# A new order of the work words in a Mamba-2 scan followed by a low-rank mixer

## The chip, the cores and the metric

The kernel runs on one core of one Trainium2 chip. Its time is the device time of one execution in microseconds; for the kernel before, three runs gave 214.86 (median), 214.03 and 215.4. The profile comes from one further execution on the chip, taken by the hardware profiler, so its span is not one of these three times.

## The reference, cut to what matters

```python
# attention: batch 4, heads 8, sequence 768, head_dim 32, state 16, chunks of 32
for c in range(nc):
    la  = log_a[:, :, sl];  cum = np.cumsum(la, axis=-1)
    L   = np.exp(cum[..., :, None] - cum[..., None, :]) * causal
    M   = einsum('bhin,bhjn->bhij', Cc, Bc) * L
    y[:, :, sl] = einsum('bhij,bhjd->bhid', M, xc) \
                + einsum('bhin,bhnd->bhid', Cc, state) * exp(cum)
    state = exp(sum(la)) * state + sum_j(Bc * xc * exp(cum[-1] - cum))
# bridge: (batch, heads, seq, head_dim) -> x of (batch, 768, 256)
# mixer: U 768x32, V 32x768, w_ch1 256x1024, w_ch2 1024x256
h  = x.T @ U @ V
u  = x + h.T
return u + relu(u @ w_ch1) @ w_ch2
```

U, V and both w arrive as float64; everything else is float32.

## The kernel before

**How the work is cut.** A batch's 768 tokens are three pairs of 128-token blocks, so there are 12 pairs over the four batches. The scan goes pair by pair; the mixer goes batch by batch, and within a batch in three blocks of 256 tokens.

**What sets the order.** The kernel is one long list of words. `PLANS[1]`, a string of 547 words (lines 40 to 72), is read by `follow` (lines 1063 to 1082) from left to right, and each word issues the instructions of one step on whatever engines the step uses. The program is under manual scheduling, so each engine runs its instructions in the order in which the words stand; waits between engines come from the data. Moving a word therefore moves its instructions in the queues of TensorE, VectorE, ScalarE, GpSimd and SyncE at once. `PLANS[0]` holds the loads that are issued first: B, C and x of the pairs 0 to 2.

**How to read a word.** In the words of the scan, the first number is an offset: -3, -2, -1 are the pairs 0 to 2 (batch 0), 0 to 2 the pairs 3 to 5, 3 to 5 the pairs 6 to 8, 6 to 8 the pairs 9 to 11. In the words of the mixer the first number is a lag: 1 is batch 0, then 0, -1 and -2 are the batches 1 to 3.

- Loads, all on SyncE's queue: `B` (B and C of a pair), `X` (x of a pair), `L` (both), `Z0` and `Z1` (U and V), `w0` and `w1` (the halves of w1's first quarter), `w2` to `w4` (its other quarters), `w5` to `w8` (the four pieces of w2). A load by `B`, `X`, `w` or `L` is held until the last VectorE instruction ahead of its word is done: `follow` sets `until[:] = [vector.last]`, and `begin` (line 195) hangs the first DMA on it. `Z` is not held.
- `c`, the conversion of float64 words to float32 (`to_fp32`, lines 402 to 436), in three passes, one for each time the word stands: two VectorE operations and one ScalarE copy; one ScalarE operation; three VectorE operations. `c0` is U and V, `c1` and `c2` are the halves of w1's first quarter, `c3` to `c5` its other quarters, `c6` to `c9` the pieces of w2. `R` refines a converted piece into three parts for products in a faster format.
- The scan: `A`, `K` (decays), `P`, `Q` (B and C scaled, into `BC`; `Q` is one block), `D`, `E` (B decayed, into `bd`), `V`, `T` (transposes of `BC` into `T` and `Cm`; from pair 6 on by VectorE's own transposes, a trip through DRAM, `squares`, and back), `g` (the products of C and B), `m`, `M` (the causal mask on them, one half each), `s` (the pair's state sums), `u` (the running state `S`), `n` (products within a chunk), `i`, `j` (products with the state), `y` (copies of the result into `yT`), `t`, `O` (the result with tokens on partitions, `ytok`; late pairs by the same kind of trip).
- The mixer: `v` spreads U and V, `p` is x.T U (line 803, copied to `pT` on line 808), `x` the product with V (line 815), `a` adds it to `yT`, `S` splits a block of u into three parts, `U` is a plain float32 product of a block with one quarter of w1 (for the first two blocks of batch 0), `f`, `e`, `h` are the first, second and third step of the same product in three parts, `d` is one piece of the product with w2, with the last sum and the store in its last pieces.
- `F` is a run of idle matmuls.

All VectorE operations go through one recording helper, so they all show as line 170. In `inter` (the words `i` and `j`), a tiny VectorE copy, `settled`, is put in ahead of the products where no earlier instruction is at hand to order them after others (`apart`).

**Where the change acts.** The words of the start run up to the first product with w1, those of the second stage until two blocks have met all of w1, then come dense products of the batches 0 and 1 with the scan of later pairs between them, then the last pairs' scan and the mixing of batch 2 (`p-1`, `x-1`, `a-1`, `S-1`), then the products of the last two batches.

Of the kernel before, what the change touches and what calls it, by code (L numbers as in the profile page):

```python
# [71 lines left out]
}


# [1041 lines left out]
```

## The time and the profile before

| | |
|---|---|
| median of three runs | 214.86 us (214.03 to 215.4) |
| span of the profiled execution | 212.4 us |
| instructions | 7511 |
| TensorE matmul | 202.9 us busy (96%) |
| TensorE weight load | 180.9 us (85%) |
| VectorE | 173.2 us (82%) |
| ScalarE | 121.0 us (57%) |
| GpSimd | 6.3 us (3%) |
| DMA | 21.43 MB, 101 GB/s on average |
| chain that ended last | TensorE 75%, VectorE 8%, issue 4%, DMA 4% of the span |

The profiled execution's own time is its span, 212.4 us; the timed runs are 2.46 us above it by their median, and contain whatever lies around the span. A busy share is a mean over stages with different limits, so the table says that TensorE is nearly always occupied, and not what each stage waits for. In the views, PE is a matmul, PEld a weight load, DVE VectorE, ACT ScalarE and SPq a transfer issued by SyncE; a row of a timeline begins with the start and the duration in microseconds, and ends with the idle time before it and what released it, where there was some.

### The profile page before, as it was taken

Reading aid. Unit: us, or ns where it says so; the run is one execution under the profiler, and the core shown is the slowest. Engines: PE = TensorE matmul, PEld = TensorE weight load, DVE = VectorE, ACT = ScalarE, POOL = GpSimd, SP = SyncE. Lnnn points to the kernel's source line nnn. Section 1 sums busy time; section 2 is a strip of 40 time slices with the busy share of each in tenths; the row PEclk is TensorE's granted clock in tenths of the full one; section 3 lists DMA queues with packets and bytes.
Section 4 is the critical chain, followed back from the end, with each engine's and each line's share of the span. In section 5 each row is a group of like instructions: output and inputs, shape, how many; then the busy total and the mean of one; then the engine's idle time right before and its main releaser. Section 6 shows DMA issues by size and latency. Waiting matters only on the chain.

```text
span 212.4 us, 7511 instructions
## 1 busy us (share of the span) xinstructions
PE 202.9 (96%) x3190; PEld 180.9 (85%) x3190; DVE 173.2 (82%) x363; ACT 121.0 (57%) x279; POOL 6.3 (3%) x22
## 2 busy tenths in 40 slices
PE   7988889999999999999999999899999999999994
PEld 5765666878979997988999999589998999999993
DVE  4299979999899999999799995777986299859941
ACT  3354668489969746285588361669713565554310
POOL 4022000000000000000000000000000000000000
PEclk9999999999999999999999999999999999999999
DMA  5997799994751488356755766626510000324354
GB/s 82 138 150 160 89 246 181 190 241 121 102 71 31 79 207 130 88 83 83 108 89 94 149 143 132 112 38 122 117 52 0 0 5 0 49 32 71 49 102 99
DMA packets 120177, 21.43 MB, mean 101 GB/s; under 512 B 110096, under 2 KB 118352, under 8 KB 120144
## 3 DMA queue, kind: packets, MB, share of 16 engines
q1 hardware_dynamic: 120144, 20.95, 53.9%
q8 instruction: 25, 0.41, 0.9%
q14 instruction: 8, 0.07, 0.2%
HBM read 14.39 MB, written 6.55 MB: 99 GB/s over the span
## 4 chain that ended last, share of the span: by engine, by line
PE 75%; DVE 8%; issue 4%; DMA 4%; ACT 3%; SPq 3%; POOL 0%; POOLq 0%; DVEq 0%; ACTq 0%
PE x L846 35%; PE z L846 28%; DMA bc<-in_B_dram 4%; SPq L196 3%; DVE words L170 2%; PE x L584 2%; PE z L739 1%; PE w L803 1%; PE x L714 1%; PE x L739 1%; DVE S L170 1%; ACT yT L759 1%; PE x L815 1%; DVE o L170 1%; DVE BC L170 1%
## 5 line engine op out<-in xcount | busy, mean ns | idle before, releaser
L170 DVE SCALAR_TENSOR_TENSOR words<-words 128x512 fp32r<-128x512 f32 (+6 forms) x60 | 39.4, 669 | 2.4 <-ACT words L420 0.8
L846 PE MATMUL x<-words,w 128*128 128x256 f32 x288 | 38.1, 280 | 0.0
L846 PEld LDWEIGHTS x<-words,w 128*128 128x128 f32 x288 | 34.9, 188 | 1.6 <-issue 1.2
L846 PE MATMUL x<-u,w 128*128 128x256 f32 x240 | 34.3, 282 | 0.0
L846 PE MATMUL z<-u,w 128*128 128x256 f32 x240 | 32.7, 278 | 0.0
L851 ACT ACTIVATE x<-x 128x512 f32<-128x512 f32 (+1 forms) x27 | 15.5, 577 | 28.2 <-PE x L846 26.4
L846 PEld LDWEIGHTS x<-u,w 128*128 128x128 f32 x240 | 30.3, 188 | 0.6 <-ACT yT L759 0.2
L846 PEld LDWEIGHTS z<-u,w 128*128 128x128 f32 x240 | 29.7, 188 | 0.1
L851 ACT ACTIVATE z<-z 128x512 f32<-128x512 f32 (+1 forms) x24 | 13.7, 574 | 12.3 <-PE z L846 10.2
L846 PE MATMUL z<-words,w 128*128 128x256 f32 x144 | 19.6, 280 | 0.0
L846 PEld LDWEIGHTS z<-words,w 128*128 128x128 f32 x144 | 17.7, 188 | 0.9 <-issue 0.9
L170 DVE SCALAR_TENSOR_TENSOR words<-x,words 128x512 fp32r<-128x512 f32 x20 | 13.6, 682 | 4.5 <-ACT words L886 4.4
L170 DVE SCALAR_TENSOR_TENSOR words<-z,words 128x512 fp32r<-128x512 f32 x20 | 13.6, 682 | 2.2 <-ACT words L886 2.2
L886 ACT ACTIVATE words<-x 128x512 fp32r<-128x512 f32 x20 | 12.0, 598 | 3.3 <-PE x L846 3.2
L170 DVE TENSOR_TENSOR yT<-x,yT 128x384 f32<-128x384 f32 (+1 forms) x15 | 9.2, 613 | 5.1 <-PE x L846 2.7
L170 DVE TENSOR_TENSOR BC<-bc,F 128x512 f32<-128x512 f32 (+2 forms) x18 | 8.7, 508 | 5.4 <-DMA bc<-in_B_dram 3.0
L886 ACT ACTIVATE words<-z 128x512 fp32r<-128x512 f32 x20 | 11.8, 597 | 1.7 <-PE x L846 1.2
L170 DVE SCALAR_TENSOR_TENSOR S<-S,kept,w 128x64 f32<-128x64 f32 x40 | 11.2, 279 | 1.7
L584 PE MATMUL x<-Cm,T 32*64 32x128 f32 x192 | 11.6, 307 | 0.6 <-DVE Cm L170 0.4
L651 ACT ACTIVATE Sm<-S,slot 128x128 f32<-128x128 f32 (+1 forms) x18 | 6.0, 385 | 9.9 <-DVE S L170 9.9
L584 PE MATMUL z<-Cm,T 32*64 32x128 f32 x192 | 10.5, 307 | 0.0
L170 DVE TENSOR_TENSOR M<-x,causal 128x256 int32<-128x256 int32 x24 | 9.1, 421 | 1.6 <-PE z L584 1.6
(152 smaller groups left out, 363.5 us busy)
## 6 DMA issues: line engine op xcount, KB each, us to landing
words<-in_moe_w_ch_dram SPq DMA_DIRECT2D x7, 512.0 KB, 5.5
squares<-w1f SPq DMA_DIRECT2D x52, 64.0 KB, 1.9
x<-in_x_dram SPq DMA_DIRECT2D x24, 128.0 KB, 4.1
out_dram<-o SPq DMA_DIRECT2D x32, 64.0 KB, 2.3
bc<-in_B_dram SPq DMA_DIRECT2D x24, 64.0 KB, 3.5
bc<-in_C_dram SPq DMA_DIRECT2D x12, 128.0 KB, 3.9
T<-squares SPq DMA_DIRECT2D x6, 256.0 KB, 4.3
ytok<-squares SPq DMA_DIRECT2D x6, 256.0 KB, 3.6
```

The source lines that it names most:

```text
L170: self.last = call(*args, **kwargs)
L196: op = nc.sync.dma_start(**kwargs)
L584: nc.tensor.matmul(out=g[r][cols, c], lhsT=s["T"][rows, 0, c, cols], rhs=s["Cm"][rows, :, :, ts(2 * c + p, Q)].rearrange("r v t i -> r v i ...
L651: nc.scalar.activation(s["Sm"][:, sl, v], s["S"][:, sl, ts(v, D)], AF.Copy, scale=slot[:, v, None])
L714: product = nc.tensor.matmul(out=y[r // 2][p][ts(v, H), c], lhsT=own[ts(r, Q)], rhs=s["T"][ts(r, Q), 1, :, ts(2 * c + p, Q)].rearrange("r ...
L739: product = nc.tensor.matmul(out=y[n][p][ts(v, Q), c], lhsT=x_sb[k][half, c, h], rhs=s["M"][half, h // 2, c, h % 2], start=fresh(k, n, p, ...
L759: nc.scalar.copy(out=yp[ts(1 - v, H), n, :, p], in_=y[n][p][ts(v, H)])
L803: nc.tensor.matmul(out=p[ts(n, H)], lhsT=UU[:, c].rearrange("p t r -> p (t r)"), rhs=ytok[b][:, c, ts(n, P)], start=(c == 0), stop=(c == N ...
L815: nc.tensor.matmul(out=h[q][:, :VS], lhsT=pT[rows], rhs=V4[rows], start=True, stop=True, skip_group_check=True)
L846: nc.tensor.matmul(out=t, lhsT=lhsT, rhs=rhs, start=start, stop=True, skip_group_check=True)
L851: nc.scalar.activation(t, t, AF.Copy, scale=1.0 + EPS)
L886: nc.scalar.activation(gs[j, i][0], t, AF.Relu, scale=NEAR)
```

## The change

The 547 words are the same, in a new order; no function is touched. U and V (`Z0`, `Z1`) are loaded later, behind the second pair's state words, and w1's first half quarter (`w0`) earlier; w1's third quarter (`w3`, `c4`) is loaded and converted ahead of its second and fourth, and `U1.0.2`, the product with it, is the first product with w1. Between the dense pieces `d0.1` and `d0.2` of batch 1 stand more words of the last pairs, and the words `p-1` and `x-1` come closer to the last of them. The pieces of the last two batches are interleaved in another way. As `i` and `j` lie differently, one more `settled` copy is issued (three, from two); otherwise every kind of instruction occurs as often as before.

The loads and conversions of the start, and the words around them (the rest of the string down to `d1.0` cut):

```diff
-        'Z1 F5 A0 Q-3.0 Q-3.1 A1 Q-3.2 F4 V-3.0.0 Q-2.1 V-3.1.5 K2 D-3 g-3 Q-2.2 Q-2.0 V-2.0.2 '
-        'Z0 m-3 M-3 F2 V-2.1.2 Q-1.2 E-1.0 s-3 Q-1.0 D-2 n-3 w0 Q-1.1 V-1.0.2 u-3 F1 V-1.1.3 s-2 '
-        'w1 i-3 g-2 u-2 j-3 y-3 F2 g-1 i-2 B3 B4 B5 w2 w3 X3 w4 X4 m-2 M-2 w5 c0 c0 m-1 B6 O-3.0 '
-        'c0 M-1 w6 E-1.1 n-2 s-1 u-1 c2 v0 w7 c1 c2 j-2 i-1 y-2 j-1 n-1 c1 y-1 P0 D0 c1 T0 c2 '
-        't-2 O-1.3 P2 X5 T0 X6 w8 P1 D2 p1.0.4 p1.4.6 c3 c3 x1 a1.0 a1.1 T1 T2 T2 T1 g0 U1.0.0 '
-        'c3 c4 c4 U1.0.1 g1 m0 M0 c5 c4 m1 M1 c5 D1 s0 u0 U1.1.0 U1.1.1 U1.1.2 i0 n0 y0 c6 c6 s1 '
-        'c5 g2 c7 u1 R2 m2 c7 U1.1.3 M2 c8 c8 c7 U1.0.2 L4 U1.0.3 i1 n1 y1 c6 R1 R0 c8 R5 c9 s2 '
-        'c9 c9 n2 d1.0 L5 R6 u2 R0 d1.1 P3 S1.2 d1.0 R7 d1.0 i2 y2 R3 t1 R1 t0 R2 R5 d1.1 R4 P4 '
...
+        'F5 A0 Q-3.0 Q-3.1 A1 Q-3.2 F4 V-3.0.0 V-3.1.5 Q-2.1 w0 Q-2.2 K2 g-3 D-3 s-3 Q-2.0 D-2 '
+        'V-2.0.2 F2 V-2.1.2 Z0 g-2 E-1.0 m-3 M-3 s-2 u-3 Q-1.2 w1 Q-1.0 V-1.0.2 Q-1.1 E-1.1 m-2 n-3 '
+        'i-3 u-2 Z1 c1 w3 B3 c1 B4 B5 M-2 i-2 n-2 c1 j-3 c2 c0 c0 X3 y-3 F1 V-1.1.3 s-1 j-2 F2 g-1 '
+        'c0 y-2 v0 t-2 u-1 O-3.0 m-1 M-1 c4 c4 c2 i-1 j-1 P0 n-1 D0 p1.0.4 y-1 c4 O-1.3 w2 p1.4.6 P1 '
+        'T0 c2 T0 w4 x1 w5 T1 a1.0 T1 a1.1 g0 U1.0.2 m0 M0 P2 X4 w6 D1 c3 s0 c3 U1.0.0 u0 g1 T2 X5 '
+        'w7 c3 w8 R0 L5 m1 D2 M1 T2 c5 c6 U1.1.0 c5 U1.0.1 s1 i0 n0 y0 c6 c5 R2 u1 U1.1.1 B6 c7 '
+        'U1.0.3 s2 c6 u2 R1 g2 R3 c7 c8 c8 U1.1.2 m2 M2 c7 R5 c8 U1.1.3 c9 n2 i2 S1.2 y2 d1.0 d1.1 '
+        'c9 i1 R4 n1 c9 L4 P3 D3 R0 T3 d1.0 d1.0 R2 y1 R3 X6 d1.0 t0 f1.2.2 P4 f1.2.0 R1 f1.2.3 '
...
```

The place of `n3` to `n5`, where a wait for a mask can arise:

```diff
-        'f0.0.1 e0.0.0 T5 f0.0.2 f0.0.3 d1.2 D4 s4 e0.0.1 u3 e0.0.2 e0.0.3 L7 L8 D5 s5 h0.0.0 i3 '
-        'n3 y3 d0.0 d0.0 u4 h0.0.1 g5 h0.0.2 u5 d0.0 d0.0 d0.0 h0.0.3 d0.0 m5 M5 d0.0 P6 d0.0 T6 '
-        'n4 S0.1 i4 y4 d0.0 D6 d0.0 d0.0 d0.0 D8 f0.1.2 P7 T7 S0.2 f0.1.3 s6 n5 i5 y5 e0.1.2 '
...
+        'f0.0.0 M4 f0.0.1 e0.0.3 d1.2 e0.0.0 e0.0.1 u5 d1.1 i3 n3 n4 i4 d0.0 y3 L8 h0.0.2 h0.0.3 '
+        'h0.0.0 y4 h0.0.1 d0.0 d0.0 d0.0 P6 S0.1 d0.0 g5 m5 d0.0 M5 f0.1.1 T6 n5 S0.2 i5 P7 y5 d0.0 '
```

The last pairs and the mixing of batch 2:

```diff
-        'd0.1 d0.2 h0.2.2 d0.1 d0.1 d0.1 d0.2 d0.2 d0.2 h0.1.1 d0.1 t4 T7 d0.0 P8 T8 s7 u7 g6 m6 '
-        'd0.1 M6 t5 d0.1 d0.2 d0.1 d0.2 d0.2 d0.2 d0.1 d0.1 d0.1 d0.1 s8 u8 n6 i6 y6 p-1 g7 T8 '
-        'd0.2 x-1 d0.1 m7 M7 n7 a-1.0 a-1.1 S-1.0 i7 y7 g8 f-1.0.2 f-1.0.3 m8 M8 n8 i8 y8 t6 t7 '
-        'S-1.1 e-1.0.2 h-1.0.2 t6 e-1.0.3 f-1.0.0 f-1.0.1 h-1.0.3 t8 f-1.1.3 e-1.0.0 e-1.0.1 '
...
+        'd0.2 d0.1 d0.2 d0.2 d0.2 T8 u6 g7 s7 d0.1 d0.0 m7 D8 M7 d0.2 d0.1 u7 d0.1 d0.1 d0.2 g6 s8 '
+        'm6 T8 M6 d0.1 d0.2 d0.2 n6 u8 d0.2 p-1 i6 x-1 n7 d0.2 i7 y6 a-1.0 a-1.1 S-1.0 y7 t6 g8 m8 '
+        'f-1.0.0 f-1.0.1 M8 e-1.0.0 n8 i8 y8 t7 S-1.1 e-1.0.1 f-1.0.2 f-1.0.3 t8 f-1.1.2 f-1.1.1 '
...
```

The order of the first loads behind the first three pairs was V, U, w0, w1, B3, B4, B5, w2, w3, X3, w4, X4, w5, B6, w6, w7, X5, X6, w8, and is w0, U, w1, V, w3, B3, B4, B5, X3, w2, w4, w5, X4, w6, X5, w7, w8, the load of pair 8, B6. The plain products with w1 stood as U1.0.0, U1.0.1, U1.1.0, U1.1.1, U1.1.2, U1.1.3, U1.0.2, U1.0.3, and stand as U1.0.2, U1.0.0, U1.1.0, U1.0.1, U1.1.1, U1.0.3, U1.1.2, U1.1.3.

35 rows, old and new, of the table PLANS are left out of this document.

## The prediction

> **What bounds the kernel now.** I read the page first (engine shares, queues), then a table of busy time by stage, then the timelines of VectorE, ScalarE and SyncE where a stage showed slack.
>
> ```profile
> span 212.4 us, 7511 instructions
> PE 202.9 (96%) x3190; PEld 180.9 (85%) x3190; DVE 173.2 (82%) x363; ACT 121.0 (57%) x279; POOL 6.3 (3%) x22
> ...
> q8 instruction: 25, 0.41, 0.9%
> ```
>
> TensorE's bar fills 96% of the span, but a bar also covers waiting of small matmuls, so the share says little before the stages are taken apart. The stages below are mine: up to the first product with w1, up to the state where all of w1 has been multiplied for two blocks, the dense middle, the hole at 130, the dense end, the tail.
>
> ```profile
> core 0: us, PE busy (x) PEld busy (x) DVE busy (x) ACT busy (x) POOL busy (x), PEclk, DMA share, GB/s
> 0.00:33.80 33.80, 29.02 (x626) 21.47 (x626) 24.72 (x78) 17.96 (x48) 6.27 (x22) 1.00 0.86 147
> 33.80:62.30 28.50, 27.87 (x502) 22.54 (x497) 26.80 (x62) 21.38 (x49) 0.00 (x0) 1.00 0.74 150
> 62.30:130.10 67.80, 67.58 (x1061) 62.42 (x1060) 62.64 (x123) 42.25 (x99) 0.00 (x0) 1.00 0.60 107
> 130.10:139.10 9.00, 8.29 (x305) 5.88 (x304) 7.19 (x16) 5.04 (x17) 0.00 (x0) 1.00 0.65 126
> 139.10:209.30 70.20, 70.14 (x709) 68.55 (x704) 51.41 (x87) 34.39 (x69) 0.00 (x0) 1.00 0.26 49
> 209.30:212.40 3.10, 0.00 (x0) 0.00 (x0) 0.40 (x1) 0.00 (x0) 0.00 (x0) 0.94 0.41 109
> ```
>
> Weight loads (second number) show density better than matmuls: 62.42 of 67.80 in the middle (92%) and 68.55 of 70.20 at the end, but 5.88 of 9.00 in the hole and 21.47 of 33.80 at the start. A new order of the same instructions can win only where TensorE is not dense: the start (bound by VectorE and the transfers, DMA share 0.86), the second stage (VectorE 26.80 of 28.50, TensorE 27.87: both near full) and the hole. The clock is 1.00 until TensorE's work ends (0.94 in the tail), so no term comes from it. The last 3.10 us belong to the last sum and store, which the new order leaves last.
>
> **The change part by part.** The 547 words are the same ones; nothing is added but one tiny copy (`settled`), as the pairs j and i lie differently. So every term is a wait or a place in a queue.
>
> *Start, on VectorE's queue.* The chain that ends at a1.0 (the first sum into the mixer's input) passes through VectorE:
>
> ```profile
> 9.95 0.29 DVE L170 TENSOR_TENSOR BC<-bc,F 128x128 f32<-128x128 f32 x1 [1.59 <-DMA bc<-in_B_dram]
> 10.16 0.60 DVE L170 TENSOR_SCALAR Cm<-w,slot 128x128 f32<-128x128 f32 x2
> ...
> 16.18 1.30 DVE L170 SCALAR_TENSOR_TENSOR S<-S,kept,w 128x64 f32<-128x64 f32 x4
> 17.40 0.14 DVE L170 COPY settled<-slot 128x1 f32<-128x1 f32 x1
> ...
> 24.86 0.69 DVE L170 TENSOR_TENSOR BC<-bc,F 128x512 f32<-128x512 f32 x1
> ...
> 29.84 1.29 DVE L170 TENSOR_TENSOR BC<-bc,F 128x512 f32<-128x512 f32 x2 [1.36 <-DMA bc<-in_B_dram]
> 31.05 0.42 DVE L170 TENSOR_TENSOR bd<-bc,FD 128x256 f32<-128x256 f32 x1
> 31.39 0.76 DVE L170 TENSOR_SCALAR words<-words 128x512 int32<-128x512 int32 x2
> 32.06 0.55 DVE L170 TENSOR_TENSOR yT<-x,yT 128x384 f32<-128x384 f32 x1
> ...
> 33.92 1.29 DVE L170 SCALAR_TENSOR_TENSOR words<-words 128x512 f32<-128x512 f32 x2
> 35.24 0.69 DVE L170 SCALAR_TENSOR_TENSOR w1f<-words 128x512 f32<-128x512 f32 x1
> ```
>
> Out of the queue ahead of a1.0 go: the 0.60 of V-3.1.5's copies, which now stand before Q-2.1 and run inside its wait of 1.59; P2 and with it the wait of 1.36 for B5 (P2 takes half of the 1.29, 0.65); D2, 0.42; c3's first pass, 0.76. Together 3.79. Into it come: c4 whole, by c3's rows 0.76 + 1.29 + 0.69 = 2.74; the `settled` copy, 0.14; and a new wait, c1's first pass for w0. Its price follows from SyncE's queue:
>
> ```profile
> 13.05 0.58 SPq L196 DMA_DIRECT2D words<-in_moe_V_dram  x1
> ...
> 17.57 0.37 SPq L196 DMA_DIRECT2D bc<-in_B_dram  x1
> ```
> ```profile
> words<-in_moe_w_ch_dram SPq DMA_DIRECT2D x7, 512.0 KB, 5.5
> ...
> words<-in_moe_w_ch_dram SPq DMA_DIRECT2D x2, 256.0 KB, 4.6
> ```
>
> w0 takes V's place at 13.05 and lands 4.6 later, at 17.65. VectorE is there after u-2, which ended at 17.40 and now ends some 0.5 sooner (the 0.60, less a little overlap), so it stands still for about 0.7, and M-2, the rest of c1, j-3, c2 and c0 queue behind it. Bounds: 0 if w0 lands before 16.9, 1.5 if it needs the 5.5 us of the larger pieces. I take 0.7, because the row is that of the same transfer. In: 3.58; out: 3.79; a1.0 starts at 31.9 instead of 32.06, and VectorE has 2.74 - 1.83 = 0.9 more of its work behind it there. U, V sooner or later costs nothing by itself: c0's last pass feeds v0, and V4 is first read by x1, some 6 us after.
>
> *Second stage.* U1.0.2 can start right behind a1.1, where U1.0.0 did (33.8), as c4 is done; U1.0.0 and U1.1.0 need c1, c2, which are done too, so c3 and c5 get their time behind dense work. VectorE's lead is then 0.9, and one more wait in front of c9 may go:
>
> ```profile
> 57.42 1.30 DVE L170 SCALAR_TENSOR_TENSOR words<-words 128x512 f32<-128x512 f32 x2 [0.80 <-ACT words L420]
> ```
>
> In the new order S-1.2 stands before c9's last pass and covers ScalarE's part of c9. But TensorE itself has only 28.50 - 27.87 = 0.63 to give here. The gain lies between 0 and 0.63; I take 0.5, as the first half of VectorE's lead is enough for it.
>
> *Middle.* 67.58 of 67.80: TensorE is full, another order gains nothing by this row. The pairs n-3, n-4 now stand back to back, and n-5 behind f0.1.1 must wait for M5, which has S0.1 before it: a wait of some 0.7 by VectorE's queue, against small waits now. I take 0, and -1 to +1 as bounds.
>
> *The hole at 130.* Here the old order has used up its dense products before the last pairs' attention and the next batch's mixing, which are chains:
>
> ```profile
> 130.13 0.43 PE L619 MATMUL w<-x,bd 64*32 64x64 f32 x24
> ...
> 131.19 0.28 PE L714 MATMUL x<-T,Sm 32*64 32x64 f32 x2
> ...
> 131.62 1.59 PE L803 MATMUL w<-ytok,UU 128*64 128x128 f32 x24
> ...
> 135.00 0.59 PE L815 MATMUL x<-V,pT 32*128 32x384 f32 x2 [0.61 <-ACT pT L808]
> ```
> ```profile
> 133.13 0.27 ACT L761 COPY yT<-x 128x128 f32<-128x128 f32 x1 [0.63 <-DVE o L170]
> ...
> 134.68 0.27 ACT L808 COPY pT<-w 128x128 f32<-128x128 f32 x1
> 135.31 0.91 ACT L551 ACTIVATE Cm<-T,slot 128x256 f32<-128x256 f32 x2 [0.36 <-DMA T<-squares]
> ```
> ```profile
> 124.20 0.71 DVE L170 STREAM_TRANSPOSE w1f<-BC 128x512 f32<-128x512 f32 x1
> ...
> 131.74 1.30 DVE L170 STREAM_TRANSPOSE o<-yT 128x512 f32<-128x512 f32 x2
> ...
> 135.95 0.56 DVE L170 TENSOR_TENSOR yT<-x,yT 128x384 f32<-128x384 f32 x1
> ...
> 137.81 0.68 DVE L170 TENSOR_TENSOR u<-yT,u 128x512 fp32r<-128x512 f32 x1
> ```
>
> At the density of the middle the 5.88 us of loads would need 5.88 / 0.92 = 6.4; the hole costs 9.0 - 6.4 = 2.6. One piece is plain: pT is ready to be copied at 133.2, but ScalarE does y6's six copies first, and these wait for VectorE's output transposes (131.74). In the new order pT's copy stands before y6; g7, s7, g6, s8 and n6 have d0.1 and d0.2 pieces between and behind them. What is left bare behind the last d0.2 is p-1, i6, x-1, n7, i7, g8: the 6.4 less s8 and n6 (131.19 - 130.13 = 1.06) and g7 (0.8, an estimate: half of p-1's 1.59, as its rows were not separated), so 4.5. The chain beside it: p-1 1.59, pT 0.27, x-1 to the first sum 0.95 (135.00 to 135.95), the four sums 1.86 (135.95 to 137.81), the far half of the split 0.68: 5.35 until f-1.0.0 can run through. Slack 0.85 instead of 2.6: a gain of 1.75. Bounds: 0 if T8's round trip is late (below), 2.6 if nothing waits.
>
> *Instruction blocks.* The order is said to follow their arrival. q8's 25 packets and 0.41 MB are blocks of 16 KB, and TensorE's loads do wait where nothing else ends the wait:
>
> ```profile
> PEld x L714 <- issue: 1.5, 5, 0.3
> ...
> PEld x L846 <- issue: 1.4, 5, 0.5
> PEld x L739 <- issue: 1.3, 3, 0.6
> ```
>
> These are 4.2 us at most over the span, mostly in waits of 0.3. I put no term on them: they lie in the start, where VectorE's chain ends last anyway, and inside stages already counted. [...]
>
> *Sum.* Start -0.2, of which nothing counts twice as U1.0.2 is tied to a1.1; second stage -0.5; middle 0; hole -1.75; end 0 (68.55 of 70.20 is dense). Together -2.4: the span goes from 212.4 to 210.0. This execution is profiled; the median of the three timed runs is 214.86, 2.46 above its span, so the forecast is 212.5.
>
> **The rivals.**
> - *The stream of transfers slips* (slower). w3 is put ahead of B3, and waits until c1's first pass is done (18.2: w0's 17.65 and some 0.6, an estimate from c3's 0.76 on twice the columns), where B3 went out at 17.57; 512 KB at 147 GB/s are 3.6 us before it. B3 leaves 1.2 later and lands 3.5 to 4.8 later, P0 (24.86) then waits to 28 or more, and D0, c4's last pass, the ytok copy, P1 and a1 stand behind it on VectorE; w2, w4 and w5 wait for these in turn, so c3 and c5 are late as well. It decides when P0 waits over 1.5. Price: 3 to 4 at U1.0.1, partly made up: +3.0, and if the hole's gain halves, 214.9 + 3.0 - 0.9 = 217. For it: DMA share 0.86. Against: VectorE now has the whole of c4's first pass and M-1 before P0, so 1 us of lateness is free.
> - *The hole stays.* T8 now takes 135.31 + 0.91 - 124.20 = 12.0 from its transposes to its Cm; in the new order about 10.5 us of TensorE's words lie between T8 and g8. If the trip takes 12.0 again, g8 and what follows it waits 1.5, and the gain falls to 0.25: 214.0. For it: T8's stores share SyncE with the outputs of d0.0, which come right behind. Against: in the old order those outputs stood before T8's stores.
> - *Blocks count.* If the 4.2 of issue waits are real and half go, 212.5 - 2.1 = 210.4. Against: the dense middle shows few of them.
>
> **How the numbers follow.** Forecast 0.37 (211.3 to 213.5), hole stays 0.30, slip 0.21, blocks 0.12. A difference under 1%, 2.1 us, is about what a measurement here cannot tell from none. Faster by over 1% (below 212.7): 0.22 of the forecast's own range and tails, the blocks' 0.12, and 0.06 from better cases of the hole: 0.42 with rounding. Slower (above 217.0): 0.18. Within: 0.40. The range takes the blocks' case at its low end less a little and the slip's at its high: 209.6 to 217.2.
>
> **What would show it.** Right: a1.0 near 31.9 with no long wait before P0; U1.0.2 near 33.8; no wait for c9; from the last d0.2 to f-1.0.0 about 5.4 us, with pT's copy ahead of y6's. Wrong: an idle VectorE before BC at 25 to 28 (slip); g8 waiting for Cm behind a landing of T (hole); a stage from 62 to 130 that lasts over 1 us longer than 67.8, which I have put at 0.

## The result, and the profile after

The new order is slower: 218.25 us against 215.13 us (medians of four executions each), a ratio of 1.015 with a 95% interval of 1.010 to 1.020. The forecast was 212.5 us, its range 209.6 to 217.2. A second comparison (a0_new, below) gave 1.019 (1.011 to 1.027). Ratios, and medians of spans further down, leave out executions more than 1.5% above the fastest of the same kernel beside them. The profiled execution's span is 216.1 us against 212.4, so 3.7 us have to be found. Both spans lie at the low end of what was timed: wherever a run lists the time and the span of one execution, they are 1.66 to 1.98 us apart. So 212.4 belongs to a time of some 214.1 us (of the 2.46 that the prediction put between span and median, some 0.7 was only this), and 216.1 to the fastest of the new order's four, 217.82.

The page of the new order, its first lines and TensorE's clock over 40 slices, in tenths of full speed:

```profile
span 216.1 us, 7539 instructions
PE 205.5 (95%) x3190; PEld 181.3 (84%) x3190; DVE 174.0 (81%) x364; ACT 121.7 (56%) x279; POOL 6.5 (3%) x22
...
PEclk9988589999999999999999999999999999999999
...
q8 instruction: 25, 0.41, 0.9%
```

One row is new: the granted clock. In the old order it was 1.00 up to the tail; here it falls in two places, from 15.0 to 18.3 us and from 21.8 to 28.6. The bars of the matmuls are 2.6 us longer (205.5 against 202.9) at the same 3190 instructions, while VectorE and ScalarE have nearly the same (174.0 against 173.2, 121.7 against 121.0). The view of busy time by stretch, of the new order and then of the old one, with the same columns as in the prediction:

```profile
10.00:15.00 5.00, 2.46 (x86) 1.60 (x77) 4.69 (x14) 1.95 (x7) 1.23 (x3) 0.99 0.99 105
15.00:18.40 3.40, 3.40 (x138) 2.39 (x122) 3.23 (x11) 1.33 (x5) 1.30 (x3) 0.51 1.03 253
18.40:21.80 3.40, 2.31 (x100) 1.84 (x92) 3.34 (x11) 1.66 (x4) 0.35 (x1) 0.99 0.59 182
21.80:28.30 6.50, 6.32 (x97) 3.91 (x96) 5.00 (x15) 2.96 (x9) 0.51 (x1) 0.50 0.88 110
28.30:33.80 5.50, 4.98 (x132) 3.81 (x131) 4.21 (x9) 3.88 (x9) 0.00 (x0) 0.97 0.71 85
```
```profile
10.00:15.00 5.00, 3.92 (x141) 2.92 (x140) 4.79 (x17) 2.16 (x8) 1.67 (x3) 1.00 1.05 130
...
18.40:21.80 3.40, 2.77 (x102) 1.95 (x108) 3.35 (x10) 2.40 (x6) 0.13 (x1) 1.00 0.61 91
21.80:28.30 6.50, 5.86 (x209) 4.56 (x191) 6.32 (x20) 4.17 (x14) 0.51 (x1) 1.00 0.81 100
```

From 21.8 to 28.3 us TensorE runs at 0.50 of its clock. Its bar is nearly full there (6.32 of 6.50) with 97 matmuls instead of 209, and it is now VectorE that waits (5.00 busy instead of 6.32). Who waits for whom is in VectorE's and ScalarE's timelines:

```profile
22.71 0.14 DVE L169 COPY settled<-slot 128x1 f32<-128x1 f32 x1
...
25.91 0.76 DVE L169 TENSOR_TENSOR M<-x,causal 128x256 int32<-128x256 int32 x2 [0.70 <-PE z L583]
...
29.47 0.15 DVE L169 COPY settled<-slot 128x1 f32<-128x1 f32 x1 [1.48 <-PE z L713]
29.58 0.69 DVE L169 TENSOR_TENSOR BC<-bc,F 128x512 f32<-128x512 f32 x1
...
35.00 0.56 DVE L169 TENSOR_TENSOR yT<-x,yT 128x384 f32<-128x384 f32 x1 [0.23 <-PE z L814]
```
```profile
27.40 0.32 ACT L1015 COPY V<-x 128x192 f32<-128x192 f32 x1 [2.47 <-PE z L1011]
```

P0 (`BC`) starts at 29.58, and not because B3 is late: ahead of it the copy `settled` waits 1.48 us for TensorE. The first sum of a1.0 starts at 35.00 instead of the old order's 32.06, and the first product with w1 follows. The rows that date the rest, from TensorE's timelines of the new and of the old order (the first product with w1, the first piece of d1.0, i7, the first product behind g8, and the last products):

```profile
36.79 0.70 PE L845 MATMUL x<-yT,w1f 128*128 128x256 f32 x2
...
57.05 1.99 PE L845 MATMUL x<-words,o 128*128 128x256 f32 x8
...
140.26 0.28 PE L713 MATMUL x<-T,Sm 32*64 32x64 f32 x2
...
141.99 1.18 PE L845 MATMUL x<-u,w 128*128 128x256 f32 x8
...
211.65 1.10 PE L845 MATMUL z<-w,words 128*128 128x256 f32 x8
```
```profile
33.84 1.99 PE L846 MATMUL x<-yT,w1f 128*128 128x256 f32 x8
...
54.76 1.99 PE L846 MATMUL x<-words,o 128*128 128x256 f32 x8
...
137.38 0.28 PE L714 MATMUL x<-T,Sm 32*64 32x64 f32 x2
...
139.11 1.06 PE L846 MATMUL x<-u,w 128*128 128x256 f32 x7
...
208.17 1.07 PE L846 MATMUL z<-w,words 128*128 128x256 f32 x8
```

The old order's first product stood at 33.84 (in the experiment b1_pt, whose start is the old one, at 33.83). Against it the new order is 2.95 us late at the first product, 2.29 at the first d1.0 (57.05 - 54.76), 2.53 at i3 (97.48 - 94.95), 2.88 at i7 and at the first product behind g8, 3.51 at the end of the last product (212.75 - 209.24), and 3.7 at the end of the span. At i3, at i7 and at the end TensorE has the same words behind it in both orders. At the first d1.0 it has not: the old order has done n1 by then, and the new one does it later (from 61.16 to 61.97), so 2.29 flatters the new order by some 0.8.

### The profile page after: what moved, and what is told of

Read it like the earlier page. It is cut to its first block, busy times and chain, and to the rows that moved or that the text cites. A ratio compares the mean times of both kernels' runs of the same rounds, so it can differ in the third digit from the quotient of the medians.

```text
span 216.1 us, 7539 instructions
## 1 busy us (share of the span) xinstructions
PE 205.5 (95%) x3190; PEld 181.3 (84%) x3190; DVE 174.0 (81%) x364; ACT 121.7 (56%) x279; POOL 6.5 (3%) x22
## 4 chain that ended last, share of the span: by engine, by line
PE 83%; DVE 6%; ACT 3%; DMA 3%; SPq 2%; issue 1%; DVEq 0%
PE x L845 36%; PE z L845 28%; PE x L583 3%; SPq L195 2%; DMA bc<-in_B_dram 2%; PE w L618 2%; PE z L738 2%; PE x L814 2%; DMA T<-squares 1%; PE x L713 1%; PE w L802 1%; PE x L738 1%; DVE BC L169 1%; DVE M L169 1%; PE w L768 1%; PE z L713 1%
## 5 line engine op out<-in xcount | busy, mean ns | idle before, releaser
L845 PE MATMUL x<-words,w 128*128 128x256 f32 x288 | 40.0, 280 | 0.0
L845 PEld LDWEIGHTS x<-words,w 128*128 128x128 f32 x288 | 35.7, 188 | 1.5 <-issue 1.2
L845 PE MATMUL z<-u,w 128*128 128x256 f32 x240 | 34.2, 280 | 0.0
L845 PEld LDWEIGHTS z<-u,w 128*128 128x128 f32 x240 | 30.4, 188 | 0.2
L845 PE MATMUL z<-words,w 128*128 128x256 f32 x144 | 21.2, 281 | 0.0
L845 PEld LDWEIGHTS z<-words,w 128*128 128x128 f32 x144 | 18.4, 188 | 0.9 <-issue 0.7
L169 DVE TENSOR_TENSOR u<-yT,u 128x512 fp32r<-128x512 f32 x10 | 6.9, 686 | 7.8 <-ACT u L839 7.6
L583 PE MATMUL x<-Cm,T 32*64 32x128 f32 x192 | 11.0, 322 | 1.4 <-ACT Cm L507 1.0
L169 DVE TENSOR_TENSOR BC<-bc,F 128x512 f32<-128x512 f32 (+2 forms) x18 | 9.9, 566 | 2.0 <-ACT F L371 1.3
L550 ACT ACTIVATE Cm<-T,slot 128x256 f32<-128x256 f32 x12 | 5.4, 500 | 9.8 <-DMA T<-squares 9.8
```

The costliest lines, as they stand in the source:

```text
L169: self.last = call(*args, **kwargs)
L550: nc.scalar.activation(s["Cm"][:, i], s["T"][:, 1], AF.Copy, scale=slot[:, i, None])
L583: nc.tensor.matmul(out=g[r][cols, c], lhsT=s["T"][rows, 0, c, cols], rhs=s["Cm"][rows, :, :, ts(2 * c + p, Q)].rearrange("r v t i -> r v i ...
L845: nc.tensor.matmul(out=t, lhsT=lhsT, rhs=rhs, start=start, stop=True, skip_group_check=True)
```

## The experiments

Each kernel was timed in turn with the old order on the same chip; ratios are to it. "First product" is the start of the first product with w1 in the profiled execution. Where single executions are named, span and mean granted clock of each belong together.

**The two orders put together, cut near 160 and 216 words**

```diff
 s1_oldstart: old order up to the first d1.0 (158 words), then the rest as in the new one
 s2_newstart: new order up to the first d1.0 (157 words), then the rest as in the old one
 q1_old84:    old order through 218 words, then the rest as in the new one
 q2_new84:    new order through 216 words, then the rest as in the old one
```

> The words of the old order up to the first d1.0, then all the remaining words in the new order. If the loss is made at the start (by TensorE's clock, or by the queue of VectorE), the granted clock stays at 1.00 through the first 35 us, the first product with w1 begins near 33.8 us, and the time is 215.1 to 215.6 us: the late part of the new order gives and takes about nothing. If the late part loses as well, the time is above 216.5; if the late part had the gain of 1.75 that was forecast for the hole, it is near 213.5.

> The words of the new order up to the first d1.0, then all the remaining words in the old order. If the loss is made at the start: clock at 0.5 in parts of 15 to 28 us, first product with w1 near 36.8, time 217.6 to 218.3 us. If the late part of the new order is what loses, 215.5 or less.

> The old order through the last words of batch 0's third block (the first 218 words), then the remaining words in the new order. If the loss is the start's: first product near 33.8 and 215.3 to 216.7 us (new hole and new wait of n4 for y3's copies about 1 us against it). If the later part loses by itself: above 217.2.

> The new order through the same place (its first 216 words), then the remaining words in the old order. If the loss is the start's: first product near 36.8 and 217 to 218.3 us. If the later part of the new order makes the loss: below 216.2.

Measured: s1 1.046 (1.038 to 1.053), s2 1.028 (1.019 to 1.037), q1 1.021 (1.014 to 1.029), q2 1.018 (1.010 to 1.026). First products at 33.87, 37.37, 34.74 and 38.86. The starts came roughly as the theory of the start had it: old words at 33.9 to 34.7, new ones at 37.4 to 38.9. The times did not, for the seams cost by themselves. The table of waits of s1 has one that neither order has:

```profile
PEld x L713 <- ACT Sm L650: 6.1, 1, 6.1
```

In that kernel u2, and its copies on ScalarE, come behind the whole of c9, and i2 needs them nearly at once. q1 shows 1.06 us for a third step (`words`) at 85.6 and 1.2 for the split. These four place the late start in the first 160 words, and say nothing on the worth of the later ones.

**Which part of the start: cut at word 39, right behind the second pair's states**

```diff
 s5_oldhead: old order through 39 words, then the rest as in the new one
 s7_newhead: new order through 39 words, then the rest as in the old one
```

> The first 39 words of the old order (through u-2, the second pair's states; U and V are loaded as early as there), then the remaining words in the new order. If the gaps of the new head between 10 and 15 us, and the low clock that follows them, make the late first product, it begins at 34 to 35.2 us and the time is 215.3 to 216.8. If the words behind the second pair's states do it (w1's third quarter ahead of the mixer's sums, w3 ahead of B3), it begins at 36 to 37.3 and the time is 217.5 to 219.5.

> The first 39 words of the new order (through i-3 and u-2), then the remaining words in the old order. The head as the cause: first product at 36 or later, time 217 to 219. The words behind it as the cause: first product at 34 to 35.2, time 215 to 216.5.

Measured: s5 1.0125 (1.002 to 1.023), first product 37.60, mean clocks 0.975 to 0.984. s7 1.007 (1.002 to 1.013), first product 35.79, and a clock of 0.999 or more in eight of ten executions. So the gaps of the new head between 10 and 15 us (TensorE's bar is 3.07 of 5.00 us there in s7's profile, at a clock of 1.00) are not enough to make the clock fall: with the new head alone it mostly stays up. With the old head and the new words behind it, it falls (0.50 from 24 to 28 us in its profile), and once already between 12 and 17 us, in the old words. The new head costs some 2 us at the first product in this combination (35.79 - 33.84), with no fall of the clock; 35.79 lies between what was expected of either cause.

**The conversion and the transfer that the change moved forward**

```diff
 v1_c4late
-... m-1 M-1 c4 c4 c2 ... p1.0.4 y-1 c4 O-1.3 ... g0 U1.0.2 m0 M0 P2 ... s0 c3 U1.0.0
+... m-1 M-1 c2 ... p1.0.4 y-1 O-1.3 ... g0 U1.0.0 m0 M0 c4 P2 ... c4 s0 c3 c4 U1.0.2
 v2_w3late
-Z1 c1 w3 B3 c1 B4 B5 M-2
+Z1 c1 B3 c1 B4 B5 w3 M-2
```

> The new order, but w1's third quarter is converted behind the mixer's first sums (three words c4 moved behind a1.1), and U1.0.0 is the first product with w1, U1.0.2 the second. If VectorE's chain ahead of the sums is what makes the first product late, c4's 2.74 us there are gone: first product 1.5 to 2.7 us sooner than in the new order (34.1 to 35.5), time 216 to 217.5, unless the next products then wait for c3 and c4. If TensorE's own chain (low clock, v0, t-2, i-1) sets it, it begins 0 to 0.7 sooner and the time is 217.8 to 219.5.

> The new order with the load of w1's third quarter moved behind those of B3, B4 and B5. If the order of the transfers counts (B3 late for P0, as one rival of the prediction had it), the time falls by 1 us or more; if not, it stays within 0.6 us of the new order's, as P0 is not waiting for B3 in its profile.

Measured: v1 1.043 (1.032 to 1.054), first product 38.03, though c4's 2.74 us are out of VectorE's queue ahead of it; the products then wait for the late conversions as well. v2 1.030 (1.022 to 1.038), first product 41.93, with this row on VectorE's timeline:

```profile
32.49 0.76 DVE L169 TENSOR_SCALAR words<-words 128x512 int32<-128x512 int32 x2 [3.93 <-DMA words<-in_moe_w_ch_dram]
```

Neither edit brings the first product forward. With c4 where it is, w3 has to go out ahead of B3; and that the transfers do not make the new order late is seen in r4 below, where P0, with the loads in the same order, runs at 27.25 without a wait for B3. v1 alone doesn't settle VectorE's chain, since its clock fell further (0.962 to 0.970); r4's first product at a full clock does.

**Idle products to hold the clock**

```diff
 s3_warm (on the new order): F6 ahead of V-2.0.2, F4 ahead of g-2, F2 ahead of i-2
 s6_warm2: as s3_warm, with F4 ahead of i-2, and F4 instead of F1 ahead of V-1.1.3
 s4_cold (on the old order): F2, F1, F2 behind V-2.0.2 left out
```

> The new order with three more runs of idle products, put where TensorE stands still anyway: six units ahead of V-2.0.2, four ahead of g-2, two ahead of i-2. Clock theory: the granted clock stays at 1.00 from 10 to 30 us, the first product with w1 begins 2 to 4 us sooner than 36.8, and the time is 215 to 216.5 us. Rival (w3 ahead of B3 and w1's third quarter ahead of the mixer's first sums make VectorE's chain longer, and the clock only falls beside it): the clock is up, but the first product still begins at 36 or later, and the time is 217.5 to 218.5.

> The new order with more idle products than the run before it had: six units ahead of V-2.0.2, four ahead of g-2, four ahead of i-2, and four instead of one ahead of V-1.1.3. Clock theory: executions whose mean clock is 0.998 or more have a span within 1.5 us of the old order's 212 to 214, and the first product with w1 begins below 35.5 us in a profile whose clock stays at 1.00 from 20 to 30 us; each stretch of 3.4 us at half clock in the start costs 1 to 2 us. Rival (VectorE's chain): 36 or later and 217.5 or more whatever the clock.

> The old order without its idle products between 12 and 25 us (F2, F1, F2 are left out; the idle products ahead of them stay). Clock theory: without them the clock falls to 0.5 somewhere between 12 and 28 us, and the time rises by 1 to 3 us to 216 to 218. If the clock stays at 1.00, the gaps of the old order are short enough by themselves, and the time is 214.5 to 215.3; then the price of the clock is not seen here. Rival: the clock falls and the time stays within 0.5 us of 215.1.

Measured in s3 (span at mean clock): 214.9 at 1.000, 218.4 at 0.992, 218.2 at 0.983, 220.4 at 0.967; in s6: 217.0 at 1.000, 219.1 and 218.0 at 0.992, 220.9 at 0.985, with a ratio of 1.019 (1.010 to 1.027). For s3 no ratio is given, as its executions lie too far apart. In both programs the execution at a full clock is the fastest, by 1 us or more. But the idle products don't hold the clock, and in s6 TensorE's timeline has a wait that neither order's profile has there, ended by nothing but the issue of the next instruction:

```profile
21.92 0.24 PE L738 MATMUL z<-M,x 64*32 64x64 f32 x1 [1.26 <-issue]
```

s4 lowers the old order's clock to 0.976 to 0.992 (0.52 from 17.5 to 24.5 us in its profile), puts its first product at 34.97, and its ratio is 1.001 (0.996 to 1.005). So the fall costs less there than the comparison can see, though not nothing: the first product of its profile is 1.1 us late, and the old order beside it wasn't always at a full clock either (0.983 to 1.000). s3 was a miss as an experiment on the first product (37.30), since its profile had the clock at 0.50 from 22 to 28 all the same.

**The mask that TensorE waits for, ahead of the conversion**

```diff
 r1_mask
-Z1 c1 w3 B3 c1 B4 B5 M-2 i-2 n-2 c1 j-3 c2 c0 c0 X3
+Z1 w3 M-2 B3 B4 B5 i-2 c1 n-2 c1 c2 j-3 c1 c0 c0 X3
 a0_new: the new order
 r4_all: r1_mask, and besides
-i3 n3 n4 i4 d0.0 y3 L8 h0.0.2 h0.0.3 h0.0.0 y4 ...
+i3 n3 d0.0 y3 L8 h0.0.2 h0.0.3 h0.0.0 d0.0 n4 i4 y4 ...
   and T8's ScalarE copies behind pT's copy (a third step of T8 behind p-1)
```

> The new order with M-2, the mask that i-2 and n-2 wait for, put ahead of c1's first pass on VectorE (and c2's first pass ahead of the settled copy of j-3). Theory: c1 ahead of M-2 leaves TensorE too little to do between 18 and 21.8 us, its clock falls to half for 6.4 us, and the chain v0, t-2, i-1, n-1, p1 runs through TensorE at that clock. Then the clock stays at 1.00 from 20 to 30 us in most executions (mean clock 0.992 or more), the first product with w1 begins 1.5 to 2.5 us sooner than in the new order beside it (near 34.5 to 35.3), and the time is 1 to 2.5 us below it. Rival (clock only a companion): first product within 0.7 us of the new order's, time within 0.6 us of it.

> The new order itself once more, beside the others on the same chip: ratio to the old order 1.010 to 1.020, mean clock 0.975 to 0.985, first product between 36.5 and 37.5.

> The mask-first edit on the new order, with two more: n4 and i4 behind two more pieces of d0.0, and T8's ScalarE copies (Cm) put behind pT's copy, so that pT no longer waits for T8's round trip through DRAM. If the three losses add up: 3 to 4 us below the new order, at or below the old order's time. If the hole gives nothing back, within 0.5 us of the mask-first kernel alone.

Measured: r1 1.018 (1.009 to 1.026), a0 1.019 (1.011 to 1.027), r4 1.0135 (1.003 to 1.024). As a cure r1 is a miss: its mean clock was 0.975 to 0.992. So is r4, which was to win back 3 to 4 us of the new order's time and won some 1.2. a0's first product, at 37.64, lies just above what was expected of it. The two profiles are worth more than the times. Up to n4 near 100 us the two programs are the same, but the clock was not, in r4 and then in r1:

```profile
22.00:24.00 2.00, 1.50 (x46) 0.91 (x45) 1.97 (x8) 1.98 (x7) 0.00 (x0) 1.00 0.77 120
24.00:26.00 2.00, 2.00 (x53) 1.50 (x53) 1.93 (x7) 0.95 (x4) 0.51 (x1) 1.00 0.53 53
26.00:28.00 2.00, 1.72 (x66) 1.30 (x69) 2.00 (x7) 2.00 (x6) 0.00 (x0) 1.00 0.76 95
```
```profile
22.00:24.00 2.00, 1.43 (x44) 0.90 (x42) 1.97 (x8) 1.78 (x6) 0.00 (x0) 0.98 0.92 142
24.00:26.00 2.00, 2.00 (x41) 1.21 (x44) 1.80 (x6) 0.80 (x3) 0.51 (x1) 0.50 0.43 40
26.00:28.00 2.00, 2.00 (x20) 1.30 (x12) 1.58 (x5) 0.79 (x3) 0.00 (x0) 0.66 0.94 114
```

One stretch of some 3.4 us at half clock, and the first product stands at 34.46 in r4 and 35.97 in r1: 1.5 us, of which 0.15 were there before the fall (the copy `settled` at 22.88 in r1, at 22.73 in r4). r4 beside the new order gives the price of the whole fall, with r1's edit in it. VectorE's rows of r4, the same instructions as those shown of the new order above:

```profile
22.73 0.14 DVE L169 COPY settled<-slot 128x1 f32<-128x1 f32 x1
...
27.14 0.15 DVE L169 COPY settled<-slot 128x1 f32<-128x1 f32 x1
27.25 0.69 DVE L169 TENSOR_TENSOR BC<-bc,F 128x512 f32<-128x512 f32 x1
...
32.67 0.56 DVE L169 TENSOR_TENSOR yT<-x,yT 128x384 f32<-128x384 f32 x1 [0.23 <-PE z L817]
```

VectorE is at the same instruction at the same time in both (22.71 and 22.73). Behind it `settled` comes at 27.14 instead of 29.47, and the sum at 32.67 instead of 35.00: 2.33 us, all of it made while the clock was at half; 0.70 and 1.48 of it are the waits for TensorE shown above, which r4 doesn't have. TensorE's own rows show the same, of r4 and then of the new order (v0's spread of V, and the transposes of t-2):

```profile
24.71 0.58 PE L1014 MATMUL x<-UV,ident 128*32 128x192 f32 x8
...
25.55 0.66 PE L771 MATMUL w<-ident,yT 128*128 128x128 f32 x4
```
```profile
25.78 0.90 PE L1011 MATMUL x<-UV,ident 128*32 128x192 f32 x8
...
27.25 1.11 PE L768 MATMUL w<-ident,yT 128*128 128x128 f32 x4
```

Two more profiles have the new order's words up to n4: a0, the new order itself, and t1 (below). Behind 18 us the clock is at half for none of the time in r4, 3.4 us in r1, 6.8 in the new order (21.8 to 28.6), 6.8 in t1 (21.2 to 28.0) and 10.2 in a0 (18.9 to 29.1), and the first products stand at 34.46, 35.97, 36.79, 37.28 and 37.64. The more of the start runs at half clock, the later it ends. One program thus varies by 0.85 us at its first product; a0 ends its last product 1.07 us behind the new order's first profile, so most of the difference between the two is made in the start.

**The later losses, one by one**

```diff
 t1_n4 (on the new order): the n4 edit of r4_all alone
 b1_pt (on the old order)
-n6 i6 y6 p-1 g7 T8
+n6 i6 p-1 y6 g7 T8
```

> The new order with n4 and i4 moved behind two more pieces of d0.0, so that y3's copies have emptied the banks before n4 needs them. If the 1.0 us that TensorE stands still at n4 is on the path, the time falls by 0.7 to 1.1 us against the new order, to 217.2 to 217.6; if it is given back later (the last pairs' chains set the end of that stretch), by less than 0.4.

> The old order with one word moved: p-1 (and with it pT's copy) ahead of y6, as the new order has it, and nothing else. The prediction's step: pT's copy no longer waits for y6's six copies, x-1 starts at 133.7 to 134.2 instead of 135.0, and the time falls by 0.5 to 1.3 us. If the wait passes on (the sums of a-1 need y6's copies, which come later by as much), it falls by less than 0.3.

t1 took TensorE's wait of 0.61 at n4 away (0.22 is left), but its executions (215.2 at a mean clock of 1.000, 218.1 at 0.984, 220.1 and 219.3 at 0.975) lie too far apart for 1 us; no ratio is given, and it doesn't settle what n4 costs. Its execution at a full clock, 215.2, and that of s3, 214.9, still lie above the old order's median of 213.3 at 0.995 or more, so the clock isn't the whole loss. b1, which moves p-1 and pT's copy ahead of y6 and nothing else, is slower: 1.007 (1.002 to 1.012). Its table of waits between 131 and 142 us says where the wait went:

```profile
PEld x L583 <- ACT yT L760: 0.8, 2, 0.4
PEld w L802 <- DMA ytok<-squares: 0.7, 1, 0.7
```

g7, ahead of x-1 in TensorE's queue, waits for y6's copies, which now come behind pT's; and p-1, earlier, waits for the landing of `ytok`. x-1 starts at 136.22, not 133.7. Of the 1.22 us against the old order, 1.00 stand ahead of the hole already (i6 at 132.19, against 131.19), made by a stop near 47.5 us that has nothing to do with this edit (see the rivals below). The first product behind g8 is 1.71 late (140.82), so the edit loses some 0.7 in the hole.

**Is there a version that beats both?**

```diff
 b2_warm (on the old order): F2 added ahead of V-2.0.2, F4 for F2 ahead of V-2.1.2, F2 for F1 ahead of V-1.1.3
 r5_warm (on r4_all): F4 ahead of V-2.0.2, F4 ahead of g-2, F2 ahead of i-2
```

> The old order with a few more idle products for TensorE: two units ahead of V-2.0.2 (new), four instead of two ahead of V-2.1.2, two instead of one ahead of V-1.1.3. If a half-clock stretch costs the old order too (its executions at a mean clock of 0.995 or more had a median span of 213.3, those at 0.988 to 0.995 one of 214.9), holding the clock brings the mean clock to 0.997 or more and the time 0.3 to 1.2 us below the old order's, a ratio of 0.994 to 0.999. If the idle products cost as much as they save: 0.999 to 1.005.

> The kernel with the mask first, n4 later and pT ahead of T8's copies, with idle products ahead of V-2.0.2 (four units), g-2 (four) and i-2 (two) besides. Clock theory: mean clock 0.992 or more in most executions and a ratio to the old order of 1.002 to 1.009, as against 1.0135 without the idle products. If the remaining loss is one of order: 1.012 or more at the same clock.

Measured: b2 0.999 (0.996 to 1.003), r5 1.014 (1.009 to 1.019). b2 has a higher clock (0.998 or more in nine of twelve executions), and the time of the old order. r5's clock fell again in its profile, behind a wait of 1.21 us for nothing but issue at 21.7, as in s6. None of these versions beats the old order.

## Why the prediction was wrong

Two steps failed, one on the clock and one on the overlap in the hole.

**The first is the sentence on the clock**, "1.00 until TensorE's work ends (0.94 in the tail), so no term comes from it". The clock was read as a given, and it changes with the order and from one execution to the next; in the start it cost 2.33 us. Over all comparisons the old order's 63 executions had a mean clock of 0.995 or more 29 times (median span 213.3 us), 0.988 to 0.995 28 times (214.4), and less 6 times; the new order's eight had 0.976 to 0.983, all of them. Behind 18 us the falls last 3.4 us in r1, 6.8 in the new order's first profile and in t1, and 10.2 in a0, and the mean clocks of the executions mostly lie near 0.976, 0.984, 0.992 or 1.000. These steps of 0.008 are what 3.4 us at half clock in 214 us come to. Why the falls have these lengths was not shown.

**Start** (forecast -0.2, first sum at 31.9): 35.00. The wait for w0 that the sum had at 0.7 did not come (c1's first pass starts at 17.97, right behind u-2; in a0 it waits 0.28). At a full clock, in r4, the first sum starts at 32.67, 0.8 later than forecast; why is not settled, as r4's edit moves VectorE's words (its VectorE waits 0.93 us at 20.06 for the landing of the next piece of w1). Of the 2.95 us at the first product 2.33 go with the half clock, by r4's rows, and 0.62 are the rest (34.46 - 33.84). The worth of r4's mask edit at a full clock was not measured by itself; on one and the same program up to there, r1 against r4, the price of 3.4 us at half clock is 1.4 to 1.5.

**Second stage** (forecast -0.5, at most -0.63): -0.66 from the first product to the first d1.0 (20.26 us instead of 20.92), but with n1 left for later. From the first product to i3, where both orders have done the same words, it is -0.42. So the sign is right, and the size of this stage by itself can't be read off. The profile that the forecast was read from is also the only one in which the old words lose so little there (see the rivals).

**Middle** (forecast 0, bounds -1 to +1): the wait came as one for a bank and not for a mask, at n4 instead of n5, by TensorE's timeline:

```profile
99.06 0.46 PE L738 MATMUL x<-M,x 64*32 64x64 f32 x32 [0.22 <-ACT yT L760]
...
100.32 0.43 PE L738 MATMUL z<-M,x 64*32 64x64 f32 x24 [0.61 <-ACT yT L758]
```

n4 stands right behind n3, and its banks are those that y3's copies have to empty first: 0.83 us, where the old order stops 0.16 for n3. That is 0.67, inside the bounds.

**The hole** (forecast -1.75) is the second step that failed. From i3 to i7 the new order loses 0.35 us; without n4's 0.67, the rest of that stretch, the hole in it, gains some 0.3. The chain beside the hole was forecast well: from p-1's start to the end of the split's far half it takes 5.57 us (135.80 to 141.37), not 5.35. What was wrong is the overlap: that the bare stretch of p-1, i6, x-1, n7, i7 and g8, 4.5 us at the density of the dense middle, would run beside that chain. In the new order the six words hold TensorE from 135.80 to 141.99, 6.19 us, and in the old one they hold it for 6.06 (i6 0.43, from 131.19; p-1 1.52, up to the next product at 133.14; and x-1, n7, i7 and g8 4.11, from 135.00 to 139.11). Their weight loads are busy for 4.14 of the 6.19 us. The rest is waiting, most of it for copies and sums on other engines, and the bar, 5.91 of the 6.19, covers it: a single 64x64 product has a bar of 0.24 us (s6's row above), and 24 of them have one of 0.43 (n4's row). The table of TensorE's waits between 130 and 152 us, of the new order:

```profile
PEld x L738 <- ACT yT L758: 0.5, 1, 0.5
PEld x L583 <- ACT yT L760: 0.4, 1, 0.4
...
PEld x L814 <- ACT pT L807: 0.3, 1, 0.3
PEld x L738 <- DVE yT L169: 0.2, 1, 0.2
```

x-1 waits 0.28 for pT, n7 0.55 for y6's copies and 0.23 for one of the sums of a-1, g8 0.39 for y7's copies: 1.45 together. In the sum the words were joined to the rest by pT alone. So the split was ready at 141.37, and TensorE came to f-1.0.0 at 141.99, behind g8.

pT's part of it has a cause that the prediction's "pT's copy stands before y6" missed. ScalarE's timeline of the new order:

```profile
136.24 0.91 ACT L550 ACTIVATE Cm<-T,slot 128x256 f32<-128x256 f32 x2 [3.69 <-DMA T<-squares]
137.05 0.62 ACT L650 ACTIVATE Sm<-S,slot 128x96 f32<-128x96 f32 x2
137.58 0.24 ACT L807 COPY pT<-w 128x128 f32<-128x128 f32 x1
```

The new order also puts T8's fetch, and its two copies on ScalarE, ahead of p-1. ScalarE waits 3.69 us for that landing, pT's copy queues behind it, and starts 0.25 us behind p-1's end (137.33). The rival "the hole stays" had this round trip, though at g8 and not here; that its gain of 0.25 comes near the 0.3 is luck. Where T8's copies were put behind pT's (r4), pT's copy starts as p-1 ends, but x-1's weight load waits 0.7 for y6's copies instead, and p-1 to the first product behind g8 takes 6.52 us (133.70 to 140.22). In the old order (b1) the wait passed on in the same way.

**The end** (forecast 0): from the first product behind g8 to the end of the last product it is 70.76 us, against 70.13. In a0 it was 70.75, but 70.28 in r1 and 72.37 in t1, with the same words, so these 0.6 are not the order's alone; they stay open.

**The rivals.** The slip of the transfers had the sign and the place, P0 waiting until 28 or later, but not the cause, as r4's P0 at 27.25 shows. Its 217 came near the measured 218.25 for a wrong reason. Of the gain from blocks the two profiles show nothing, with 25 packets of instructions in both; other runs show some. In six of the seven profiles whose second stage has the old words (s1, q1, s7, s4, b1, b2), TensorE stops for 0.70 to 1.68 us at the products of g2, and nothing but the next issue ends it. s1's table of waits shows it at the weight load:

```profile
PEld z L583 <- issue: 2.0, 1, 2.0
```

The seventh is the profile that the prediction was read from, and in the 13 with the new words there, edited or not, this stop is not seen. So the new order seems to save some 1 us that the old order loses in most profiled executions, and that the ledger of these two spans can't show. Whether it is a block of instructions that TensorE waits for there, no run shows.

**The sum, as it came out, on the spans:** +2.33 clock, +0.62 rest of the start, -0.42 from there to i3, +0.67 n4, some -0.3 to i7 (the hole among it), +0.63 the end, and +0.2 in the tail: 3.7. Against the forecast span of 210.0 that is 6.1 more, of which the clock is 2.3 and the stretch from i3 to i7 2.1 (+0.35 instead of -1.75). Still open is what exactly makes the clock fall. The new words behind the second pair's states make it common (mean clocks of 0.975 to 0.984 in all of s5's executions, 0.999 or more in eight of s7's ten), one mask put ahead is not enough to prevent it (0.975 to 0.992 in r1), and the same program falls or doesn't from one execution to the next (t1: 1.000, 0.984 and twice 0.975).

## What to carry to other kernels

A reordering that adds no work can still change TensorE's clock: here the mean clock was 0.976 to 0.983 in all eight executions of the new order, and 0.995 or more in 29 of the old one's 63. When costing such a change, look at where it leaves TensorE less to do (from 10 to 15 us, ahead of the first fall, its bar is 2.46 of 5.00 us, against 3.92 in the old order), and give a half clock a term wherever TensorE, and not VectorE, would be the chain (1.4 to 1.5 us for a fall of 3.4 us in r1). How little is too little was not found here: in r4 the bar is 2.62 of those 5.00 us, and the clock stayed at 1.00. One profile is one execution: a stop (that at g2 is in six profiles of seven) or a fall may be missing from the one that a forecast is read from, so profile the old kernel several times. A copy that is moved ahead of one queue neighbour may land behind another, as pT's did behind T8's copies and the 3.69 us that these waited: read the whole queue of its engine in the new order, the fetches that those neighbours wait for, and the bank that the consumer needs next. Words that are to run beside a chain may wait for it, for its copies and for the banks that these empty (1.45 us of TensorE's time in the new hole, 0.83 at n4): list what each of them waits for before taking them at the density of another stage; taking out one link of its chains (b1) showed nothing but the next. And compare two orders only at marks where the same words are done.

## What was not expected of the hardware

The clock fell without a long pause. In the new order's first profile the stretch ahead of the second fall, 18.4 to 21.8 us, has TensorE's bar at 2.31 of 3.40, and its longest wait there is 0.84 us; in r4 the same stretch was at 2.20 and the clock stayed at 1.00. (In t1 TensorE waits 1.51 us for the mask M-2 near there, and in a0 its bar is 0.60 of 2.00 us from 18 to 20.) What a stretch of 3.4 us at half clock cost here depended on who was the chain. The one from 15.0 to 18.3 us cost nothing that VectorE's rows show (`settled` at 22.71, against 22.73 in r4 at a full clock); the one in r1, where VectorE waits for TensorE (1.07 us, ahead of the copy `settled` at 28.65), cost 1.4 to 1.5 us. And idle products meant to prevent the fall did not: in s6 and r5 a stop of 1.26 and of 1.21 us that only issue ended came just ahead of it. Whether the added products made that stop was not shown.
